# Mamba2 SSD and a low-rank mixer in one kernel: the first batch's products in another order, V loaded packed, and identity products in TensorE's first waits

## The chip, the cores and the metric

The kernel runs on one core of a Trainium2 chip. The metric is the device time of one execution in microseconds (us). The engines are named as the profile names them: PE is TensorE, PEld its weight load, DVE is VectorE, ACT is ScalarE, POOL is GpSimd, and SP issues the loads and stores.

## The reference

Two stages, cut to what matters. Inputs: x is (4, 8, 768, 32), a is (4, 8, 768), B and C are (4, 8, 768, 16); U, V and the two weight matrices of the mixer come as float64.

```python
# stage 1: a state-space scan per batch and head, chunk by chunk
L = exp(cum[:, None] - cum[None, :]) * causal        # cum: running sum of log a
y = ((C @ B.T) * L) @ x  +  (C @ state) * exp(cum)
state = exp(sum(log_a)) * state + (B * decay).T @ x
# stage 2: tokens x channels, x is (4, 768, 256)
u = x + ((x.T @ U) @ V).T                            # U 768x32, V 32x768
out = u + relu(u @ w_ch1) @ w_ch2                    # w_ch1 256x1024, w_ch2 1024x256
```

## The kernel before

A batch is cut into six chunks of 128 tokens, and these into three pairs; there are four batches, so twelve pairs, numbered 0 to 11. For each pair k the code has a row of small functions, and the order in which they are called is the order of every engine's queue: nothing reorders it later.

- `prep(k)` (L285): B and C times their decays, on DVE (Bs, Cs). `turn(k, c)` (L318): four TensorE transposes of Bs and Cs for one chunk, and ACT's copy of them to T. `gram(k)` (L330): C B^T, 16 products in four row groups at a time, into the tile `g`, which has only one buffer. `mask(k)` (L341): the causal mask over g on DVE, giving M, two instructions.
- `decayed(k)` (L305) on POOL gives bd; `state(k)` (L351): TensorE products of bd and x into A; `update(k)` (L370): the state S on DVE, and on POOL its spread form `wide`.
- `ychannel(k)` (L391): y as state term (L404, T and wide) plus chunk term (L412, x and M), into the single buffer `y`, copied by ACT to yT. `ytokens(k, c, n)` (L420): y turned back to tokens by TensorE, copied to ytok.
- The mixer of a batch (L433) is a list of pieces: `project` (L438, the U products, which add up over the chunks), `mixed` (L451, V products into g and DVE's add to yT, L460), 16 `up` pieces (L462; half the tokens and 128 of the 1024 hidden columns each, four passes of L467, then a relu) and six `down` pieces (L474). `some(n)` calls the next n pieces.

The TensorE works on float32; a full product shows as two passes, a transpose as one. The PSUM tiles are `w` with three buffers, `g` and `y` with one each.

U, V and the weights arrive as float64, read as pairs of 32-bit words. `to_fp32` (L241) turns them into float32 in two halves: e and top on DVE with rest and power on ACT, then three DVE instructions. `convert(n)` takes the next n halves of a list in the order U, V, four parts of w1, four of w2; `convert_ahead()` takes the first half of one weight and the second half of the one before. Thus their places in DVE's and ACT's queues are written out by hand as well. V is loaded four times over, into 32 partitions each: the rows of V4 are what the V products need (L130 to L132).

Loads stand in SP's queue in the order of L124 to L146: a, B and C of pair 0, U, x of pair 0, B and C of pair 1, x of pair 1, B and C of pair 2, V, the first part of w1, x of pair 2, and so on.

The first batch (pairs 0 to 2) has no other mixer to run beside it; its order is written out at L524 to L567, and that of the mixer of batch 0 beside pairs 3 and 4 at L570 to L597. From pair 3 on a loop (L602) sets the order.

Of the kernel before, what the change touches and what calls it, by code (L numbers as in the profile page):

```python
# [9 lines left out]
FP32 = mybir.dt.float32  # L10
# [10 lines left out]
def kernel(  # L21
# [27 lines left out]
    nc = tc.nc  # L49
    P = 128  # L50
# [38 lines left out]
    def load_bc(k):  # L89
        b, q = pairs[k]  # L90
        bc = bc_sb[k] = raw.tile([P, 2, 2, NH, N], FP32, tag="bc", name="bc")
        for c in range(2):
            sl = ts(2 * q + c, P)
            nc.sync.dma_start(out=bc[:, 0, c], in_=B[b, :, sl, :].rearrange("h s n -> s h n"))
            nc.sync.dma_start(out=bc[:, 1, c], in_=C[b, :, sl, :].rearrange("h s n -> s h n"))
# [7 lines left out]


    U_sb = const.tile([P, NC, RK], FP32)
    V4 = const.tile([P, HS], FP32)
    w1 = const.tile([P, NCB, DF], FP32)
    w2 = const.tile([P, NM, DM], FP32)
# [16 lines left out]
    load_words(U_sb, U2.rearrange("(c p) r -> p c r", p=P))  # L125
    load_x(0)
    load_bc(1)
    load_x(1)
    load_bc(2)
    t = words_of(V4[:, None])  # L130
    for q in range(4):
        nc.sync.dma_start(out=t[ts(q, RK)], in_=V2[:, ts(q % 2, S)])  # L132
    quarter = WCOLS // NCB
    for k in range(DF // quarter):
        load_words(w1[:, :, ts(k, quarter)],
# [41 lines left out]
    bias = const.tile([P, 1], FP32)  # L177
    nc.vector.memset(bias, -896.0 * 2.0 ** 23)


    la = const.tile([P, NB, NC, NH], FP32)
    R = NB * NH * NC // 2
    la_ps = bank("w", 2, R)
    for g in range(2):
        nc.tensor.transpose(out=la_ps[:, g], in_=a_sb[:, g], identity=ident[:R, :R])
    for b in range(NB):
        g, o = divmod(b * NH * NC, R)
        nc.vector.tensor_scalar(
            out=la[:, b].rearrange("p c h -> p h c"),
            in0=la_ps[:, g, o:o + NH * NC].rearrange("p (h c) -> p h c", h=NH),  # L190
            scalar1=1e-6, scalar2=1.0, op0=ALU.max, op1=ALU.min)
# [83 lines left out]
    bds = [const.tile([P, 2 * NH, 2, N], FP32, name=f"bd{i}") for i in range(2)]  # L275
    for t in bds:
        nc.gpsimd.memset(t, 0.0)
    st = {}
    yT, ytok = {}, {}

# [37 lines left out]
    def turn(k, c):  # L318

        s = st[k]  # L320
        tp = bank("w", 4, P)
        for i, name in enumerate(("Bs", "Cs")):
            flat = s[name].rearrange("p h v n -> p (h v n)")
            for g in range(2):
                nc.tensor.transpose(out=tp[:, 2 * i + g], in_=flat[:, ts(2 * c + g, P)],  # L325
                                    identity=ident)
        s["T", c] = T = att.tile([P, 4, P], FP32, tag="T", name="T", bufs=4)
        nc.scalar.copy(out=T, in_=tp)  # L328

    def gram(k):  # L330
# [183 lines left out]
    def some(n):  # L514
        for _ in range(min(n, len(pieces))):
            pieces.pop(0)()

    one, others = slice(0, 1), slice(1, NB)
    yT[0] = mix.tile([P, NCB, S], FP32, tag="yT", name="yT")
    ytok[0] = mix.tile([P, NC, DM], FP32, tag="ytok", name="ytok")  # L520
# [1 line left out]
    project = pieces.pop(0)  # L522

    decays(one)  # L524
    prep(0, 2)
    turn(0, 0)
    turn(0, 1)
# [2 lines left out]
    convert(1)  # L530
    gram(0)
    state(0)
    mask(0)
    prep(1)
    update(0)
    decayed(1)
    turn(1, 0)
    turn(1, 1)
    convert(1)
    ychannel(0)  # L540
    gram(1)
    state(1)
    prep(2)
    mask(1)
    decayed(2)
    turn(2, 0)
    turn(2, 1)
    update(1)
    ytokens(0, 0, 2)
    project(0, 2)  # L550
    convert(1)
    gram(2)
    ychannel(1)
    state(2)
    mask(2)
    update(2)
    convert(1)
    ytokens(1, 0, 2)
    project(2, 4)
    convert(2)  # L560
    ychannel(2, True)
    ytokens(2, 0, 1)
    project(4, 5)
    ytokens(2, 1, 1)
    project(5, 6)
    convert(1)
    some(1)  # L567


    some(1)  # L570
    convert_ahead()
    some(2)
    decays(others)
    keep(others)
    convert_ahead()
    some(4)
    convert_ahead()
    some(3)
    convert_ahead()
    some(2)  # L580
    prep(3)
    decayed(3)
    convert_ahead()
    some(1)
    turn(3, 0)
    turn(3, 1)
    some(1)
    convert_ahead()
    some(1)
    convert_ahead()  # L590
    gram(3)
    state(3)
    mask(3)
    update(3)
    some(1)
    prep(4)
    decayed(4)  # L597
    assert not halves
# [66 lines left out]
```

## Time and profile before

| | us |
|---|---|
| median of 3 runs | 272.89 (272.67 to 273.1) |
| the profiled execution | 275.54 |
| its span, first to last instruction | 273.8 |
| TensorE busy | 254.0 (93% of the span) |
| DVE busy | 102.2 (37%) |
| ACT busy | 68.6 (25%) |
| POOL busy | 30.3 (11%) |

The profile comes from one execution. Its page has the busy time of each engine, the span in slices, and the chain that ended last: at each step the work that released it, followed back from the end. TensorE carries 90% of that chain. The clock that the throttle granted to TensorE is given per stretch as a share of 2.4 GHz; 0.50 is 1.2 GHz.

### The profile page before, as it was taken

What the parts mean: (1) busy time and instruction counts of PE and PEld (TensorE: products, weight loads), DVE (VectorE), ACT (ScalarE), POOL (GpSimd) and SP (SyncE); (2) the same over time, 40 slices, a digit from 0 to 9 for tenths busy, and PEclk for the clock granted to TensorE, in tenths of its full rate; (3) what the DMA queues carried; (4) which work ended last, traced back from release to release, by engine and by line L of the source; (5) the groups of instructions that cost most, each with busy time, mean ns of one, the idle gap of its engine ahead of it and who ended that gap; (6) DMA issues with size and microseconds to landing.
All of it is one profiled execution on the core that took longest, in us unless ns stands there. A gap on an engine that the chain in (4) does not pass through costs nothing.

```text
span 273.8 us, 5204 instructions
## 1 busy us (share of the span) xinstructions
PE 254.0 (93%) x2250; PEld 191.2 (70%) x2250; DVE 102.2 (37%) x194; ACT 68.6 (25%) x143; POOL 30.3 (11%) x53
## 2 busy tenths in 40 slices
PE   2878779997799999999999999999999999999994
PEld 1857536564688887666778887666688876558883
DVE  3487943997443353063430413161600121120000
ACT  5314436674202200313221101222111101211110
POOL 4031100000640330012110300010000000000000
PEclk9999977999799999999999999999999999999999
DMA  6999747999983100100000010100000101000011
GB/s 96 119 188 258 130 162 126 117 89 119 111 93 45 60 4 0 57 2 0 2 1 2 4 56 0 60 2 0 2 0 0 60 0 57 2 0 0 0 60 57
DMA packets 81463, 14.66 MB, mean 54 GB/s; under 512 B 76000, under 2 KB 79264, under 8 KB 81440
## 3 DMA queue, kind: packets, MB, share of 16 engines
q1 hardware_dynamic: 81440, 14.33, 32.5%
q8 instruction: 18, 0.29, 0.5%
q14 instruction: 5, 0.04, 0.1%
HBM read 11.17 MB, written 3.15 MB: 52 GB/s over the span
## 4 chain that ended last, share of the span: by engine, by line
PE 90%; DVE 3%; ACT 3%; issue 1%; DVEq 0%; ACTq 0%
PE w L467 31%; PE w L483 30%; PE y L412 5%; PE g L338 5%; PE w L325 5%; PE y L404 4%; PE w L479 3%; PE w L445 2%; PE w L427 2%; PE g L456 1%; DVE M L347 1%; PE w L362 1%; ACT ytok L430 1%; DVE Bs L297 1%; ACT L214 0%
## 5 line engine op out<-in xcount | busy, mean ns | idle before, releaser
L467 PE MATMUL w<-yT,w 128*128 128x384 f32 x256 | 89.4, 502 | 0.9 <-DVE yT L460 0.7
L483 PE MATMUL w<-w,gT 128*128 128x256 f32 x384 | 86.9, 379 | 0.0
L483 PEld LDWEIGHTS w<-w,gT 128*128 128x128 f32 x384 | 71.1, 190 | 8.7
L467 PEld LDWEIGHTS w<-yT,w 128*128 128x128 f32 x256 | 48.3, 195 | 33.1 <-issue 3.3
L347 DVE TENSOR_TENSOR M<-g,causal 128x1024 int32<-128x1024 int32 x24 | 28.2, 1219 | 34.5 <-PE g L338 34.5
L472 ACT ACTIVATE gT<-w 128x384 f32<-128x384 f32 x40 | 19.6, 490 | 57.9 <-PE w L467 57.9
L485 ACT COPY o<-w 128x256 f32<-128x256 f32 x24 | 8.9, 372 | 90.9 <-PE w L483 90.9
L470 DVE TENSOR_SCALAR gT<-w 128x384 f32<-128x384 f32 x24 | 13.4, 557 | 44.5 <-PE w L467 44.3
L386 POOL TENSOR_TENSOR wide<-S,rmask 128x256 f32<-128x256 f32 x20 | 12.8, 655 | 141.8 <-DVE S L381 93.4
L430 DVE COPY ytok<-w 128x512 f32<-128x512 f32 x9 | 6.2, 689 | 33.0 <-PE w L427 33.0
L328 ACT COPY T<-w 128x512 f32<-128x512 f32 x24 | 13.6, 588 | 19.7 <-PE w L325 19.4
L325 PE MATMUL w<-ident,Bs 128*128 128x128 f32 x48 | 10.3, 301 | 6.9 <-DVE Bs L297 6.9
L338 PE MATMUL g<-T 32*128 32x128 f32 x384 | 15.4, 301 | 0.0
L460 DVE TENSOR_TENSOR yT<-g,yT 128x384 f32<-128x384 f32 x16 | 7.8, 549 | 20.2 <-PE g L456 20.2
L412 PE MATMUL y<-M,x 128*32 128x128 f32 x384 | 14.8, 299 | 0.5 <-ACT yT L416 0.5
L338 PEld LDWEIGHTS g<-T 32*128 32x128 f32 x384 | 13.0, 203 | 2.9 <-issue 2.8
L325 PEld LDWEIGHTS w<-ident,Bs 128*128 128x128 f32 x48 | 6.6, 152 | 9.9 <-issue 7.0
L412 PEld LDWEIGHTS y<-M,x 128*32 128x32 f32 x384 | 10.8, 119 | 2.6 <-ACT yT L416 0.8
L404 PEld LDWEIGHTS y<-T,wide 128*128 128x128 f32 x80 | 11.0, 202 | 1.5 <-issue 0.2
L404 PE MATMUL y<-T,wide 128*128 128x128 f32 x80 | 11.8, 290 | 0.0
L418 ACT COPY yT<-y 128x512 f32<-128x512 f32 x11 | 6.4, 586 | 19.7 <-PE y L412 19.7
L325 PE MATMUL w<-ident,Cs 128*128 128x128 f32 x48 | 10.3, 300 | 0.5 <-DVE Cs L297 0.5
(71 smaller groups left out, 166.7 us busy)
## 6 DMA issues: line engine op xcount, KB each, us to landing
words<-in_moe_w_ch_dram SPq DMA_DIRECT2D x8, 512.0 KB, 5.7
x<-in_x_dram SPq DMA_DIRECT2D x24, 128.0 KB, 3.9
out_dram<-o SPq DMA_DIRECT2D x8, 384.0 KB, 2.5
bc<-in_B_dram SPq DMA_DIRECT2D x24, 64.0 KB, 4.0
bc<-in_C_dram SPq DMA_DIRECT2D x24, 64.0 KB, 3.7
words<-in_moe_V_dram SPq DMA_DIRECT2D x4, 96.0 KB, 3.3
words<-in_moe_U_dram SPq DMA_DIRECT2D x1, 192.0 KB, 3.6
a_sb<-in_a_dram SPq DMA_DIRECT2D x1, 96.0 KB, 2.1
```

Of the source, the lines that this page charges most:

```text
L325: nc.tensor.transpose(out=tp[:, 2 * i + g], in_=flat[:, ts(2 * c + g, P)], identity=ident)
L328: nc.scalar.copy(out=T, in_=tp)
L338: nc.tensor.matmul(out=g_ps[:, r, c, g], lhsT=T[rows, g], rhs=T[rows, 2 + g], start=True, stop=True, skip_group_check=True)
L347: nc.vector.tensor_tensor(out=M[:, :, c].bitcast(INT32), in0=g_ps[:, :, c].bitcast(INT32), in1=causal[:, None, None, :].to_broadcast(sh), ...
L386: nc.gpsimd.tensor_tensor(out=wide, in0=new[:, :, None, :].to_broadcast(wide.shape), in1=rmask[:, None, :, None].to_broadcast(wide.shape), ...
L404: nc.tensor.matmul(out=y[:, c, g], lhsT=wide[:, g].rearrange("p r d -> p (r d)"), rhs=s["T", c][:, 2 + g], start=fresh, stop=False, skip_g ...
L412: nc.tensor.matmul(out=y[ts(r, Q), c, g], lhsT=x_sb[k][:, c, 4 * g + r], rhs=s["M"][:, r, c, g], start=False, stop=True, skip_group_check= ...
L430: copy(out=ytok[b][:, c:c + n].rearrange("p c (g d) -> p c g d", g=2), in_=t)
L467: nc.tensor.matmul(out=g, lhsT=w1[:, n, ts(m, P)], rhs=uT[:, n, ts(k, HS)], start=(n == 0), stop=(n == NCB - 1))
L470: nc.vector.tensor_relu(gT[k][:, m], g)
L472: nc.scalar.activation(gT[k][:, m], g, AF.Relu)
L483: nc.tensor.matmul(out=o, lhsT=gT[k][:, m, ts(j, P)], rhs=w2[:, m], start=False, stop=(m == NM - 1), skip_group_check=True)
```

## The change

The order of the first batch is written anew. C B^T of a pair (`gram`) now stands ahead of the preceding pairs' y; y of pair 0 comes behind the transposes of pair 2, and y of pairs 1 and 2 behind the C B^T of pair 2. The U products (`project`) stand behind the last y. V is loaded once, as four quarters of its columns on four groups of 32 partitions (Vq, half the bytes), converted in that form, and spread to V4's layout by two TensorE products with a 0/1 matrix (`twice`, made by POOL from the identity) and an ACT copy (`spread`). Its load stands ahead of those of pair 2's B and C and of pair 1's x. A function `warm(n)` issues n products of the identity with itself into a tile that nothing reads; it is called four times, with 3, 2, 7 and 8. The tile T has six buffers instead of four. Two more conversions stand ahead of the mixer's add, and behind it the `up` pieces and the conversions are grouped otherwise.

```diff
-    load_x(1)
-    load_bc(2)
-    t = words_of(V4[:, None])
-    for q in range(4):
-        nc.sync.dma_start(out=t[ts(q, RK)], in_=V2[:, ts(q % 2, S)])
+    t = words_of(Vq[:, None])
+    for q in range(4):
+        nc.sync.dma_start(out=t[ts(q, RK)], in_=V2[:, ts(q, HS)])
+    load_bc(2)
+    load_x(1)
...
+    def warm(n, tag="w"):
+        t = bank(tag, P) if tag == "w" else bank("g", 4, 4 * P)[:, 0, :P]
+        for _ in range(n):
+            nc.tensor.matmul(out=t, lhsT=ident, rhs=ident, start=True, stop=True)
+    warm(3, "g")
     la = const.tile([P, NB, NC, NH], FP32)
...
         nc.tensor.transpose(out=la_ps[:, g], in_=a_sb[:, g], identity=ident[:R, :R])
+    warm(2, "g")
...
+    twice = const.tile([P, 2, 2, 2 * RK], FP32)
+    for j in range(2):
+        nc.gpsimd.tensor_copy(
+            out=twice[:, :, j].rearrange("p i (a r) -> p i a r", a=2),
+            in_=ident.rearrange("p (a i r) -> p i a r", a=2, i=2))
...
+    def spread():
+        v = bank("w", 2, HS // 2)
+        for i in range(2):
+            nc.tensor.matmul(out=v[:, i], lhsT=twice[:, i], rhs=Vq, start=True, stop=True)
+        nc.scalar.copy(out=V4, in_=v)
...
     decays(one)
+    warm(7, "g")
     prep(0, 2)
...
     state(0)
+    warm(8)
     mask(0)
...
-    convert(1)
-    ychannel(0)
     gram(1)
+    convert(2)
     state(1)
     prep(2)
-    mask(1)
-    decayed(2)
     turn(2, 0)
     turn(2, 1)
+    mask(1)
     update(1)
+    decayed(2)
+    ychannel(0)
+    gram(2)
+    state(2)
+    convert(2)
+    update(2)
     ytokens(0, 0, 2)
+    ychannel(1)
+    mask(2)
+    spread()
+    convert(1)
+    ychannel(2)
+    convert(1)
     project(0, 2)
+    ytokens(1, 0, 2)
+    ytokens(2, 0, 2)
     convert(1)
-    gram(2)
-    ychannel(1)
-    state(2)
-    mask(2)
-    update(2)
-    convert(1)
-    ytokens(1, 0, 2)
     project(2, 4)
-    convert(2)
-    ychannel(2, True)
-    ytokens(2, 0, 1)
-    project(4, 5)
-    ytokens(2, 1, 1)
-    project(5, 6)
+    project(4, 6)
     convert(1)
     some(1)
-    some(1)
-    convert_ahead()
-    some(2)
+    for _ in range(3):
+        some(2)
+        convert_ahead()
     decays(others)
     keep(others)
...
     gram(3)
     state(3)
     mask(3)
     update(3)
-    some(1)
+    some(2)
     prep(4)
```

In TensorE's queue at the program's start stood before (la are the logs of a, ref0 and ref1 the matrices of the decay sums):

```order
L185 MATMUL w_225<-ident_197,a_sb_72 128x96 x2
L209 MATMUL w_248<-la_224,ref0_214 128x48
L209 MATMUL w_248<-la_224,ref1_215 128x48
L325 MATMUL w_260<-ident_197,Bs_254 128x128 x2
L325 MATMUL w_260<-ident_197,Cs_255 128x128 x2
```

and now stands

```order
L185 MATMUL g_225<-ident_198 128x128 x3
L193 MATMUL w_230<-ident_198,a_sb_72 128x96 x2
L185 MATMUL g_233<-ident_198 128x128 x2
L218 MATMUL w_259<-la_229,ref0_215 128x48
L218 MATMUL w_259<-la_229,ref1_216 128x48
L185 MATMUL g_265<-ident_198 128x128 x7
L340 MATMUL w_279<-ident_198,Bs_273 128x128 x2
L340 MATMUL w_279<-ident_198,Cs_274 128x128 x2
```

so three identity products come first, two stand behind the transposes of a, and seven between the decay sums and the first transposes of Bs.

In TensorE's queue between the state products of pairs 1 and 2 and the second U product stood before:

```order
L404 MATMUL y_362<-T_272,wide_337 128x128 x2
L412 MATMUL y_362<-M_328,x_85 32x128 x16
L338 MATMUL g_382<-T_350 128x128 x8
L338 MATMUL g_382<-T_357 128x128 x8
L362 MATMUL w_399<-x_93,bd1_242 32x32 x16
L325 MATMUL w_424<-ident_197,Bs_416 128x128 x2
L325 MATMUL w_424<-ident_197,Cs_417 128x128 x2
L325 MATMUL w_431<-ident_197,Bs_416 128x128 x2
L325 MATMUL w_431<-ident_197,Cs_417 128x128 x2
L427 MATMUL w_448<-ident_197,yT_245 128x128 x4
L445 MATMUL w_454<-ytok_246,U_sb_74 32x128 x8
L338 MATMUL g_471<-T_429 128x128 x8
```

and from the state products of pair 1 on stands now:

```order
L377 MATMUL w_415<-x_104,bd1_250 32x32 x16
L340 MATMUL w_436<-ident_198,Bs_432 128x128 x2
L340 MATMUL w_436<-ident_198,Cs_433 128x128 x2
L340 MATMUL w_443<-ident_198,Bs_432 128x128 x2
L340 MATMUL w_443<-ident_198,Cs_433 128x128 x2
L419 MATMUL y_464<-T_291,wide_365 128x128 x2
L427 MATMUL y_464<-M_356,x_86 32x128 x16
L353 MATMUL g_484<-T_441 128x128 x8
L353 MATMUL g_484<-T_448 128x128 x8
L377 MATMUL w_501<-x_109,bd0_249 32x32 x8
L442 MATMUL w_526<-ident_198,yT_256 128x128 x4
L419 MATMUL y_532<-T_385,wide_456 128x128 x2
```

The state term (L404, now L419) and chunk term (L412, now L427) of y(0) moved from ahead of C B^T of pair 1 to behind the transposes of pair 2; g of pair 2 (g_484) comes ahead of y(1) (y_532), and no U product stands here any more.

In DVE's queue around the mask of pair 2 (M_519 before, M_554 now) stood before:

```order
L347 TENSOR_TENSOR M_420<-g_382,causal_239 128x4x256 x2
L381 SCALAR_TENSOR_TENSOR S_438<-S_339,kept_237,w_399 128x32 x2
L381 SCALAR_TENSOR_TENSOR S_443<-S_438,kept_237,w_399 128x32 x2
L257 TENSOR_SCALAR e_463<-words_101 128x384
L259 TENSOR_SCALAR top_464<-words_101 128x384
L347 TENSOR_TENSOR M_519<-g_471,causal_239 128x4x256 x2
L381 SCALAR_TENSOR_TENSOR S_522<-S_443,kept_237,w_510 128x32 x2
L264 SCALAR_TENSOR_TENSOR rest_466<-top_464,rest_466 128x384
L266 SCALAR_TENSOR_TENSOR power_465<-words_101,power_465 128x384
L268 SCALAR_TENSOR_TENSOR V4_75<-rest_466,power_465 128x384
L257 TENSOR_SCALAR e_544<-words_106 128x512
L259 TENSOR_SCALAR top_545<-words_106 128x512
```

and now stands:

```order
L362 TENSOR_TENSOR M_450<-g_387,causal_247 128x4x256 x2
L396 SCALAR_TENSOR_TENSOR S_453<-S_367,kept_245,w_415 128x32 x2
L396 SCALAR_TENSOR_TENSOR S_458<-S_453,kept_245,w_415 128x32 x2
L273 SCALAR_TENSOR_TENSOR rest_410<-top_408,rest_410 128x192
L275 SCALAR_TENSOR_TENSOR power_409<-words_94,power_409 128x192
L277 SCALAR_TENSOR_TENSOR Vq_75<-rest_410,power_409 128x192
L266 TENSOR_SCALAR e_513<-words_107 128x512
L268 TENSOR_SCALAR top_514<-words_107 128x512
L396 SCALAR_TENSOR_TENSOR S_521<-S_458,kept_245,w_501 128x32 x2
L362 TENSOR_TENSOR M_554<-g_484,causal_247 128x4x256 x2
L273 SCALAR_TENSOR_TENSOR rest_516<-top_514,rest_516 128x512
L275 SCALAR_TENSOR_TENSOR power_515<-words_107,power_515 128x512
```

so the second half of V's conversion, the first half of w1's first part and the last state update come ahead of the mask of pair 2.

## Rows read from the trace of the kernel before

**Rows 1.** Windows: stretch, length, each engine's busy us, PE clock, DMA share, GB/s.

```profile
75.00:273.80 198.80, 194.91 (x1644) 149.97 (x1636) 51.51 (x91) 34.23 (x73) 16.91 (x25) 1.00 0.09 22
```

**Rows 2.** Chain of work, the up products of batch 0 to its first down piece.

```profile
38.55 6.82 PE w L467 x12
...
46.99 13.17 PE w L467 x40
60.15 0.87 PE w L325 x8
...
71.30 0.76 PE y L404 x4
72.06 1.87 PE y L412 x32
73.92 1.49 PE g L338 x32
...
75.80 0.37 PE w L479 x2
```

**Rows 3.** Chain of work in order of time (start us, us, what), first batch.

```profile
6.88 1.97 PE w L325 x8
...
10.41 2.07 PE g L338 x32
...
15.60 2.05 PE w L325 x8
17.65 0.85 PE y L404 x4
18.51 1.79 PE y L412 x32
20.30 1.10 PE g L338 x32
...
26.18 1.09 PE y L404 x8
27.27 1.05 PE y L412 x32
...
33.12 0.69 PE y L412 x16
```

**Rows 4.** Windows of 2 us, the granted clock behind the POOL column.

```profile
42.00:44.00 2.00, 2.00 (x5) 1.09 (x4) 0.49 (x1) 1.18 (x3) 0.00 (x0) 0.50 0.38 94
...
72.00:74.00 2.00, 2.00 (x37) 1.52 (x36) 0.00 (x0) 0.04 (x2) 0.68 (x2) 0.50 1.34 138
```

**Rows 5.** Timeline: copy, conversion on ACT, and the wait ahead of pair 4's transposes.

```profile
29.68 0.59 ACT L430 COPY ytok<-w 128x512 f32<-128x512 f32 x1 [0.75 <-PE w L427]
...
37.06 0.72 ACT L262 ACTIVATE power<-e,bias 128x512 int32<-128x512 int32 x1
...
63.79 1.17 PE L338 MATMUL g<-T 32*128 32x128 f32 x32
...
65.63 2.35 DVE L347 TENSOR_TENSOR M<-g,causal 128x1024 int32<-128x1024 int32 x2
...
69.50 0.41 PE L325 MATMUL w<-ident,Bs 128*128 128x128 f32 x2 [2.65 <-DVE Bs L297]
```

**Rows 6.** Timeline (start us, us, engine, line), decay sums and loads.

```profile
4.17 1.09 PE L209 MATMUL w<-la,ref 128*128 128x48 f32 x4 [0.61 <-ACT la L193]
...
9.05 1.46 SPq L102 DMA_DIRECT2D x<-in_x_dram  x2
...
13.83 2.00 SPq L132 DMA_DIRECT2D words<-in_moe_V_dram  x4
```

**Rows 7.** Issues of loads, landing us at the end: second half of pair 1's x.

```profile
x<-in_x_dram SPq DMA_DIRECT2D x1, 128.0 KB, 4.3
```

**Rows 8.** Windows: DVE from mask(0) to mask(2), and what followed mask(2).

```profile
12.50:26.25 13.75, 10.20 (x201) 8.26 (x200) 11.51 (x20) 4.50 (x8) 3.77 (x6) 1.00 1.04 220
28.57:31.69 3.12, 2.02 (x27) 1.59 (x28) 2.99 (x8) 1.95 (x4) 0.77 (x1) 1.00 0.63 83
```

More of the change, by code (lines that the diff above doesn't have):

```diff
@@ L105 @@
     U_sb = const.tile([P, NC, RK], FP32)
+    Vq = const.tile([P, HS // 2], FP32)
     V4 = const.tile([P, HS], FP32)
@@ L326, in turn @@
                                     identity=ident)
-        s["T", c] = T = att.tile([P, 4, P], FP32, tag="T", name="T", bufs=4)
+        s["T", c] = T = att.tile([P, 4, P], FP32, tag="T", name="T", bufs=6)
         nc.scalar.copy(out=T, in_=tp)
@@ L538 @@
     turn(1, 1)
-    convert(1)
-    ychannel(0)
     gram(1)
+    convert(2)
     state(1)
     prep(2)
-    mask(1)
-    decayed(2)
     turn(2, 0)
     turn(2, 1)
+    mask(1)
     update(1)
-    ytokens(0, 0, 2)
+    decayed(2)
[4 more added lines that the diff above has]
+    update(2)
+    ytokens(0, 0, 2)
+    ychannel(1)
[4 more added lines that the diff above has]
+    convert(1)
     project(0, 2)
+    ytokens(1, 0, 2)
+    ytokens(2, 0, 2)
     convert(1)
-    gram(2)
-    ychannel(1)
-    state(2)
-    mask(2)
-    update(2)
-    convert(1)
-    ytokens(1, 0, 2)
-    project(2, 4)
-    convert(2)
-    ychannel(2, True)
-    ytokens(2, 0, 1)
-    project(4, 5)
-    ytokens(2, 1, 1)
-    project(5, 6)
+    project(2, 4)
+    project(4, 6)
     convert(1)
     some(1)
-    some(1)
-    convert_ahead()
-    some(2)
+    for _ in range(3):
+        some(2)
+        convert_ahead()
     decays(others)
     keep(others)
[L575 to L578, printed above, removed]
+    some(2)
     convert_ahead()
@@ L583 @@
     convert_ahead()
-    some(1)
+    some(2)
     turn(3, 0)
@@ L589 @@
     some(1)
-    convert_ahead()
     gram(3)
@@ L594 @@
     update(3)
-    some(1)
+    some(2)
     prep(4)
```

## The prediction

> **What bounds the kernel now.** I began with long stretches of the span. From 75 us on TensorE is busy 194.91 of 198.80 us at the full clock [rows 1]. Only DVE's conversions and the first batch stand before that, so the change can only move the moment at which this dense part begins; in before the first `down` piece (L479) starts at 75.80 [rows 2].
>
> Next comes the chain of waits of the first batch [rows 3]. Eight transposes take 1.97 and 2.05 us there, a C B^T group (32 passes of L338) 2.07, a y group of 32 passes of L412 1.79. Behind 20.3 the same work takes 1.10 (L338) and 1.05 (L412), and eight transposes 0.87 [rows 2, 3]. The clock column shows 1.00 from the start, but these durations are those of the lower level (1.2 GHz against 2.4), so I go by durations. TensorE had worked almost without a gap from 15.60 when they changed. The clock falls twice more: the column shows 0.50 at 42 to 44 and at 72 to 74 [rows 4]. Before the first fall lay the small steps and copies between the last y, which ended at 33.81, and the first L467 at 38.55 [rows 2, 3]; before the second TensorE had waited 2.65 us for one operand [rows 5].
>
> So before 75.8 four things are lost: a late start of the `up` products (38.55), their half clock, the wait at 69.50, and the half clock behind that.
>
> **The change part by part.** *The identity products* are two passes each. A full 128-column pass at half clock costs 0.85/4 = 0.213 us (L404) [rows 3], so a product 0.43. The three and the two lie ahead of operands that come later anyway (the first decay product starts at 4.17) [rows 6]; they push it by 0.2 at most, hidden since ACT is still loading its table then and takes the decays later. The seven stand between the decay products, which end at 5.26 [rows 6], and the first transposes, which start at 6.88 [rows 3]: 7 x 0.43 = 3.0 us, to 8.3 at half clock. If the clock rises among them they end at 7.6. I take 8.0, a step that TensorE runs 1.1 later than now, paid back by the transposes at 0.87 instead of 1.97, the four decay pairs of `keep` (1.56 now, 10.41 - 8.85) at about 0.9 and L338 at 1.10: gram(0) ends at 11.0 instead of 12.48. The eight products of the second burst lie behind state(0), where TensorE waits for DVE until 15.60: after gram(0) ends at 12.48 come mask(0) (a pair of L347 is 2.35) [rows 5] and 0.77 to the first transpose. At full clock, 8 x 2 x 0.136 (L404 26.18) = 2.2 us, they cost nothing; at half clock, 3.4 us, up to 1.0.
>
> The Trainium skill ("TensorE: Matmul & The Clock Gate", Part 1) says that the ramp to the full clock costs less than 1% of a typical kernel's span, which would be 2.7 us here. The rows don't agree: the first batch alone has lost 1.10 + 1.18 (transposes), 0.97, 0.30 and 0.74 us to the half clock, 4.3 in all, and my sum goes by them.
>
> *Loads.* On SP's queue x1 moves behind V and the loads of bc2. Now x1 is issued from 9.05 to 10.51, bc2 to 13.8, V in 2.00 us after it [rows 6]. In the new order x1 is issued from 9.05 + (1.0 to 2.0 for V, half as many bytes) + 3.3 for bc2 = 13.4 to 14.4, its second half 0.7 later, and lands 4.3 after that [rows 7]: 18.4 to 19.4. state(1) needs it, and stands in TensorE's queue behind gram(1) and ahead of turn(2). Turn(1) can start at 11.0 + 2.35 + 0.77 = 14.1; with its transposes 0.87, the copy of T 0.6 (as ytok's of the same shape) [rows 5] and L338 1.10 gram(1) ends near 16.7. **So a new wait of some 2 us for x1 appears**, queued ahead of all of the third pair's work. It is as long as what took the clock down at 69.5, so whether the clock stays up over it decides much.
>
> *The order of the first batch.* y(0) goes behind turn(2), y(1) and y(2) behind gram(2), all U products behind the last y. DVE's chain from mask(0) to mask(2): 11.51 busy us now; ahead of mask(2) come, in addition, the V half, the first half of w1's first words and the last update, 2.99 us as they are now [rows 8]; V packed saves up to half of its part (0 to 1.6). From mask(0) at 11.1: mask(2) starts at 24.0 to 25.6 and ends, 2.35 later, at 26.4 to 28.0; I take 27.3. TensorE's own chain from x1: 18.4 + 0.39 (32 state passes, 75.41 to 75.80) = 18.8, turn(2) 0.87, y(0) 0.55 + 1.05, gram(2) 1.10, state(2) 0.2, ytokens(0) half of 0.87, y(1) 1.09 + 1.05, the V spread 4 x 1.5 x 0.136 = 0.8: 25.9 at full clock; with turn(2), y(0) and gram(2) at half clock 1.1 + 1.0 + 1.0 more, 29.0, and 29.3 with the later bound of x1's landing partly under DVE's chain. y(2) starts between 27.3 and 29.3, I take 28.3, the middle.
>
> *From y(2) to the first up product.* y(2) itself 1.09 + 1.05. In before the last y ends at 33.81 and the first L467 starts at 38.55: 4.74 us of copies, U products, h and the add [rows 2, 3]. In the new order y(2) is not split, so whole copies of 0.59 [rows 5] take the place of halves, and in ACT's queue the two conversions of w1's second words stand ahead of the ytok copies (1.4 us, the second of the pair is the 0.72 row) [rows 5]; the U products of pairs 0 and 1 run under these. I add 0.8: 5.5 us, between 4.7 and 6.7. First up product at 28.3 + 2.14 + 5.5 = 36.0. The conversions that DVE now has between mask(2) and the add (two second halves, two first halves) are some two stretches like the 2.99 one [rows 8]: 27.3 + 6.0 = 33.3, ahead of the add at 35.4, so they cost nothing. **First term: 38.55 - 36.0 = 2.55.**
>
> *The ups.* The first 12 passes took 6.82, the next 40 took 13.17, that is 3.95 for 12 [rows 2]. With the full clock kept through the handover: **2.87**.
>
> *The wait at 69.50.* gram(3) ends at 64.96, but mask(3) starts at 65.63 only, since the last conversion is still on DVE; TensorE then waits 2.65 for Bs [rows 5]. The change puts two up products there instead of one (4 x 13.17/40 = 1.32 more cover), and DVE reaches that point some 3 us further ahead in its conversions, so mask(3) starts 0.5 earlier: **1.8**; 0.85 of the wait is left.
>
> *Behind it*, with 0.85 instead of 2.65 of idling the clock should stay: L404 0.76 - 0.55, L412 1.87 - 1.05, L338 1.49 - 1.10 [rows 2, 3]: **1.43**.
>
> Sum: 2.55 + 2.87 + 1.8 + 1.43 = 8.65 us. The profiled execution took 275.54 us (span 273.8), 1% over the 272.89 of the runs; it would take 266.9, and the runs 272.89 - 8.65 = **264.2**.
>
> **Rivals.** (1) *The clock is up by the first transposes and survives the x1 wait.* Then y(2) starts at 26.5 to 27.3 and the ups at 34.6: 10.05 us, 262.8. For: with the bursts TensorE's early waits are filled. Against: the 2 us at state(1).
>
> (2) *The identity products don't do what they say*: the clock stays low through them. Then turn(0) starts at 8.3, gram(0) ends near 14.0, the eight products end at 18.1, and turn(1) starts there, 2.5 later than now; x1 costs nothing then. gram(1) ends at 21.6, mask(1) at 24.2, mask(2) at 29.8; ups at 29.8 + 7.6 = 37.4, first term 1.1: 265.7. For: seven and eight products are 3 us each, and the rise in before needed more work than that. The Trainium skill (the same page and part) says that the number of products at the lower clock changes from run to run of one kernel; no row here shows a second run, and the sum does not use it.
>
> (3) *The clock falls in the handover all the same.* TensorE still waits there for the ytok copies, for pT and for the add. For: that is what it did in before; against: two wait-and-copy rounds fewer. The second term goes: 267.1. Together with (2): 268.6.
>
> (4) *Slower.* The x1 wait takes the clock down and it stays down to the ups. All work from turn(2) to h at half clock: 1.1 (turn(2)) + 1.0 (y(0)) + 1.0 (gram(2)) + 0.2 + 0.4 + 2.1 (y(1)) + 0.8 + 2.1 (y(2)) and about 2 for the handover's products = 10.6 on top of rival 1's start, ups at 45.2, the ups' second term lost, and only 1.8 + 1.43 won: -6.65 + 3.2, that is 3.4 slower, 276.3. It turns into a loss once the ups start later than 38.55 + 3.2 = 41.8 at half clock. Against: y(1), spread and y(2) are 5 us of full products in a row, as at 15.60 to 20.3.
>
> **How the numbers follow.** Forecast 0.45 (263 to 265.5), rival 1 0.15, rival 2 0.15, rival 3 0.17, rival 4 0.06; 0.02 for losses and gains that cancel out. The range goes from 261.8 (rival 1 with the handover at 4.7) to 268.6 (rivals 2 and 3 together). About 0.2% is what a measurement of this kernel can tell from no change. Faster 0.92, same 0.02, slower 0.06.
>
> **What would show it.** The first eight transposes near 0.9 us from about 8; gram(0) ended by 11; a wait of 1 to 3 us of state(1) for x1; mask(2) ended at 26.4 to 28.0 and y(2) behind it; the first up product at 34.6 to 37.4 with passes of 0.33; a wait below 1.2 ahead of turn(4); first `down` product near 67. Wrong if the ups start after 38.5, if they run at 0.64 a pass, or if the last wait is again over 2 us.

## The result and the profile after

The changed kernel takes 265.75 us (median of four executions: 264.68, 265.0, 266.49, 266.68) against 273.0 of before beside it (272.67 to 273.19): 0.973 of it, 95% interval 0.969 to 0.978, so 7.25 us faster. The prediction was 264.2 with a range of 261.8 to 268.6: the range holds the time, which is 1.55 us above the point.

The profiled execution took 264.68 us (span 263.0). Its page begins:

```profile
span 263.0 us, 5281 instructions
## 1 busy us (share of the span) xinstructions
PE 251.1 (95%) x2294; PEld 192.2 (73%) x2294; DVE 100.7 (38%) x194; ACT 67.6 (26%) x142; POOL 30.6 (12%) x55
...
PEclk9999999999999999999999999999999999999999
```

TensorE has 44 instructions more than before and is busy 95% of a shorter span; the row of its clock shows no stretch below full speed. Line numbers have moved: the transposes are L340 (L325 before), C B^T L353 (L338), y L419 and L427 (L404, L412), the `up` products L482 (L467), the first `down` pieces L494 and L498 (L479 begins them before), the identity products L185, the state products L377, the V spread L537.

The timeline of TensorE in the first batch (start us, us, engine, line, operation, count, and in brackets the idle time ahead with what ended it) answers [rows 3]:

```profile
4.98 2.78 PE L185 MATMUL g<-ident 128*128 128x128 f32 x14
7.60 0.38 PE L340 MATMUL w<-ident,Bs 128*128 128x128 f32 x2
...
9.44 1.17 PE L353 MATMUL g<-T 32*128 32x128 f32 x32
...
13.79 0.41 PE L340 MATMUL w<-ident,Bs 128*128 128x128 f32 x2 [0.80 <-DVE Bs L312]
...
17.99 0.33 PE L377 MATMUL w<-x,bd 128*32 128x32 f32 x16 [1.37 <-DMA x<-in_x_dram]
18.68 0.33 PE L377 MATMUL w<-x,bd 128*32 128x32 f32 x16 [0.36 <-DMA x<-in_x_dram]
18.95 0.44 PE L340 MATMUL w<-ident,Bs 128*128 128x128 f32 x2
...
26.30 1.13 PE L419 MATMUL y<-T,wide 128*128 128x128 f32 x8
```

A pair of transposes takes 0.38 us from 7.60 on: by the durations the clock rose among the seven identity products (the column of the clock shows 1.00 all along), and the work that ran at half of it before now takes what it takes later in the program. The new wait, state(1) for x1, is there (1.37 and 0.36), and the clock stays up behind it. The chain of waits (start us, us, what) shows what y(2) stands on and answers [rows 2]:

```profile
22.16 0.48 POOL bd L326
...
22.68 0.33 PE w L377 x16
...
25.51 0.85 PE w L537 x4
26.35 1.08 PE y L419 x8
27.43 1.05 PE y L427 x32
...
33.92 8.01 PE w L482 x24
...
61.12 0.88 PE w L340 x6
61.99 0.45 PE y L419 x4
62.44 1.01 PE y L427 x32
63.45 1.10 PE g L353 x32
...
64.94 0.37 PE w L494 x2
```

y(2) (L419, L427) starts behind the V spread (L537): TensorE works without a gap from state(2) at 22.68 to the end of y(2) at 28.48, and state(2) had to have `bd`, which POOL finished at 22.64. The first `up` product starts at 33.92 instead of 38.55; 24 passes take 8.01 (12 took 6.82 before); what follows turn(4) runs at 0.45, 1.01 and 1.10 instead of 0.76, 1.87 and 1.49; and the first `down` piece starts at 64.94 instead of 75.80. These 10.86 us are the whole difference of the two profiled executions (275.54 - 264.68). They split into 4.63 (start of the ups), 2.82 (6.82 - 12 x 8.01/24), 1.87 (wait ahead of turn(4), 2.65 in [rows 5], 0.78 now, below) and 1.56 (behind it), 10.88 in all. From there on the two kernels do the same.

The timeline of TensorE and DVE shows that wait, and two places of the first batch (mask(2), and the add ahead of the first `up` product):

```profile
60.19 0.41 PE L340 MATMUL w<-ident,Bs 128*128 128x128 f32 x2 [0.78 <-DVE Bs L312]
...
23.76 2.34 DVE L362 TENSOR_TENSOR M<-g,causal 128x1024 int32<-128x1024 int32 x2
...
33.31 1.95 DVE L475 TENSOR_TENSOR yT<-g,yT 128x384 f32<-128x384 f32 x4 [0.91 <-PE g L471]
```

The medians differ by 7.25 only, because executions of either kernel come in kinds, by the mean granted clock recorded for them: two of after at 1.00 (264.68, 265.0) and two at 0.993 and 0.994 (266.49, 266.68); those of before lie between 271.8 and 274.2 or, at 0.976 to 0.979, above 275.1. The profiled one of before is of the last kind. Where these kinds come from is part of the experiments. Below, an execution "at 1.00" is one with that recorded clock.

### The profile page after: what moved, and what is told of

The parts are those of the page before. It is cut to its first block, busy times and chain, and to the rows that moved or that the text cites. A ratio compares the mean times of both kernels' runs of the same rounds, so it can differ in the third digit from the quotient of the medians.

```text
span 263.0 us, 5281 instructions
## 1 busy us (share of the span) xinstructions
PE 251.1 (95%) x2294; PEld 192.2 (73%) x2294; DVE 100.7 (38%) x194; ACT 67.6 (26%) x142; POOL 30.6 (12%) x55
## 4 chain that ended last, share of the span: by engine, by line
PE 87%; SPq 4%; DVE 3%; issue 1%; DMA 1%; ACT 1%; POOL 1%; DVEq 0%
PE w L498 32%; PE w L482 31%; PE y L427 4%; PE g L353 4%; PE y L419 3%; PE w L340 3%; PE w L494 3%; PE w L460 2%; SPq L95 2%; PE w L442 2%; DVE M L362 1%; PE g L471 1%; DMA bc<-in_B_dram 1%; PE w L377 1%; SPq L94 1%
## 5 line engine op out<-in xcount | busy, mean ns | idle before, releaser
L482 PE MATMUL w<-yT,w 128*128 128x384 f32 x256 | 86.6, 490 | 1.1 <-DVE yT L475 0.7
L498 PE MATMUL w<-w,gT 128*128 128x256 f32 x384 | 86.9, 379 | 0.0
L498 PEld LDWEIGHTS w<-w,gT 128*128 128x128 f32 x384 | 71.1, 190 | 8.7
L482 PEld LDWEIGHTS w<-yT,w 128*128 128x128 f32 x256 | 47.0, 190 | 31.3 <-DVE yT L475 1.5
L401 POOL TENSOR_TENSOR wide<-S,rmask 128x256 f32<-128x256 f32 x20 | 12.6, 645 | 128.3 <-DVE S L396 88.6
L353 PE MATMUL g<-T 32*128 32x128 f32 x384 | 14.1, 283 | 0.2 <-ACT T L343 0.2
L353 PEld LDWEIGHTS g<-T 32*128 32x128 f32 x384 | 11.8, 186 | 2.9 <-issue 2.3
L427 PE MATMUL y<-M,x 128*32 128x128 f32 x384 | 13.0, 276 | 0.0
L419 PEld LDWEIGHTS y<-T,wide 128*128 128x128 f32 x80 | 10.3, 191 | 1.4 <-issue 0.2
L419 PE MATMUL y<-T,wide 128*128 128x128 f32 x80 | 10.9, 276 | 0.0
L427 PEld LDWEIGHTS y<-M,x 128*32 128x32 f32 x384 | 9.8, 109 | 1.4
L340 PE MATMUL w<-ident,Bs 128*128 128x128 f32 x48 | 9.3, 275 | 1.6 <-DVE Bs L312 1.6
L326 POOL TENSOR_TENSOR bd<-bc,FD 128x256 f32<-128x256 f32 (+1 forms) x12 | 7.4, 619 | 25.6 <-ACT kept L247 20.3
L340 PE MATMUL w<-ident,Cs 128*128 128x128 f32 x48 | 9.3, 275 | 0.6 <-DVE Cs L312 0.5
```

Source lines behind the costliest of these rows:

```text
L353: nc.tensor.matmul(out=g_ps[:, r, c, g], lhsT=T[rows, g], rhs=T[rows, 2 + g], start=True, stop=True, skip_group_check=True)
L401: nc.gpsimd.tensor_tensor(out=wide, in0=new[:, :, None, :].to_broadcast(wide.shape), in1=rmask[:, None, :, None].to_broadcast(wide.shape), ...
L419: nc.tensor.matmul(out=y[:, c, g], lhsT=wide[:, g].rearrange("p r d -> p (r d)"), rhs=s["T", c][:, 2 + g], start=fresh, stop=False, skip_g ...
L427: nc.tensor.matmul(out=y[ts(r, Q), c, g], lhsT=x_sb[k][:, c, 4 * g + r], rhs=s["M"][:, r, c, g], start=False, stop=True, skip_group_check= ...
L482: nc.tensor.matmul(out=g, lhsT=w1[:, n, ts(m, P)], rhs=uT[:, n, ts(k, HS)], start=(n == 0), stop=(n == NCB - 1))
L498: nc.tensor.matmul(out=o, lhsT=gT[k][:, m, ts(j, P)], rhs=w2[:, m], start=False, stop=(m == NM - 1), skip_group_check=True)
```

## Experiments

Experiments 1 to 4 ran beside one set of runs of before (273.19), 5 to 8 beside another (275.19), 9 and 10 beside a third (273.0), 11 and 12 beside a fourth (272.67). Experiments 9 to 12 ran on another chip than 1 to 8. Where medians are set against the 265.75 of after, that is over several sets; the lowest executions of before agree over them (271.81 to 271.94). In the second set four of the seven executions of before are at 0.979, so a ratio to its median is some 0.8% lower than it would be in the others.

**1. Without the identity products.**

```diff
-    warm(3, "g")
-    warm(2, "g")
-    warm(7, "g")
-    warm(8)
```

> The changed kernel without its twenty identity products; all else as in it. Theory A (they bring the full clock to the first batch): the first transposes run at about 1.97 us for eight again, the first mask starts near 12.4 instead of 10.68, and the up products start near 36 instead of 33.9; time 267.5 to 268.5. Rival (DVE and the loads set the first batch, the clock there costs nothing): 265 to 266, as the changed kernel.

266.51 us (266.44 to 268.15), 0.976 of before (0.970 to 0.982). TensorE in the timeline:

```profile
10.31 2.09 PE L351 MATMUL g<-T 32*128 32x128 f32 x32
...
15.57 0.66 PE L338 MATMUL w<-ident,Bs 128*128 128x128 f32 x2 [2.58 <-DVE Bs L310]
...
17.55 2.09 PE L351 MATMUL g<-T 32*128 32x128 f32 x32
19.57 0.66 PE L375 MATMUL w<-x,bd 128*32 128x32 f32 x32
...
35.73 2.20 PE L480 MATMUL w<-yT,w 128*128 128x384 f32 x6 [0.68 <-DVE yT L473]
```

Both C B^T groups are at half clock (2.09), the full clock comes at 21, and the wait for x1 is gone, since TensorE is late itself. The ups start 1.81 us later than in after. So the products bring 1.8 us between the two profiled executions (266.49 - 264.68), which both keep the clock afterwards, and 0.76 between the medians: 266.51 lies between what the two theories expected. All four executions are at 0.998 here, so none lost the clock later, while two of after's four are at 0.993 and 0.994; the medians set these kinds against each other. The larger part of the gain is the rest of the change.

**2. The identity products alone, in before.**

```diff
 (before)
+    warm(3, "g")
+    warm(2, "g")
+    warm(7, "g")
+    warm(8)
```

> The kernel before with the four bursts of identity products and nothing else of the change. Theory A: the first mask starts near 10.7 instead of 12.5; pair 2's B and C, which land near 17, take back a part; the old order of the y and U products keeps the rest of its waits: 271 to 272, at least two thirds of the gain then come from the new order. Rival (the identity products are the main part): 268 or less.

271.12 us (268.89 to 272.76), 0.990 of before (0.986 to 0.994). gram(0) runs at 9.78 and the ups start at 35.15, 3.4 earlier than in before, but their first 12 passes take 5.79 and the wait ahead of turn(4) is 2.65 as it was. Windows of TensorE (stretch, length, busy us of PE, PEld, DVE, ACT, POOL, the clock, DMA share, GB/s):

```profile
36.00:38.00 2.00, 2.00 (x5) 1.09 (x4) 2.00 (x6) 0.00 (x0) 0.00 (x0) 0.50 1.01 384
...
66.00:68.00 2.00, 2.00 (x10) 2.00 (x10) 0.96 (x1) 1.02 (x2) 2.00 (x3) 0.50 0.97 100
```

Both falls of the clock that [rows 4] show are still there, the first of them shorter (0.50 to 38.5 instead of 44, some 3.4 us instead of 6.8). That they go altogether belongs to the new order. Here, in the old one, the products alone bring the ups 3.4 us forward, nearly twice what they bring in the new one.

**3. x1 ahead of V on the queue** (and V's first conversion half moved behind update(1)).

```diff
     load_bc(1)
+    load_bc(2)
+    load_x(1)
     t = words_of(Vq[:, None])
...
-    load_bc(2)
-    load_x(1)
```

> The changed kernel with the loads in the order B and C of pair 2, x of pair 1, V, and the first half of V's conversion moved behind the state update of pair 1. Theory A (DVE's chain sets y of pair 2, TensorE's wait for x of pair 1 is covered by it): the wait of the state products for x (1.37 + 0.36 us) falls below 0.3, the up products start 0 to 0.5 earlier, 265 to 266. Rival (the wait for x is on the path): 1.5 us less, 263.5 to 264.5.

266.39 us (264.73 to 267.47), 0.973 (0.967 to 0.979). state(1) doesn't wait any more (it starts at 17.85), and little comes of it: turn(2) waits for DVE (0.40) and state(2) for POOL (0.70). In the profiled execution the clock rose some 2 us later than in after, mask(0) starts 1.30 later (11.98) and the ups 0.79 later (34.71); from mask(0) to y(2) it is 0.5 us shorter, about what the conversion half that was moved takes on DVE (0.42). The wait for x1 lies beside a chain of DVE (mask(1), update) and POOL (`wide`, `bd`) that state(2) waits for. At 1.00 the one execution is as long as after's (264.73).

**4. One `up` product ahead of turn(4) instead of two** (the other goes ahead of gram(3)).

```diff
-    some(1)
+    some(2)
     gram(3)
...
     update(3)
-    some(2)
+    some(1)
     prep(4)
```

> The changed kernel with one up piece instead of two between the state update of pair 3 and the products of pair 4, the other one ahead of C B^T of pair 3. Theory A: TensorE's wait for Bs of pair 4 grows by one piece, 1.3 us, and the clock may fall behind it: 267 to 268.5. Rival (the wait ends with DVE, which starts earlier when the piece is moved ahead): no change, 265 to 266.

268.41 us (267.64 to 269.85), 0.981 (0.976 to 0.987): 2.66 more than after. TensorE's timeline, and a window (columns as in 2):

```profile
58.40 1.56 PE L482 MATMUL w<-yT,w 128*128 128x384 f32 x4
62.02 0.64 PE L340 MATMUL w<-ident,Bs 128*128 128x128 f32 x2 [2.06 <-DVE Bs L312]
```

```profile
62.00:64.00 2.00, 1.69 (x7) 1.32 (x8) 1.92 (x2) 0.27 (x1) 2.00 (x3) 0.51 1.20 145
```

The wait grows from 0.78 to 2.06, that is by about the 1.3 us of the four passes moved (4 x 0.334), and the clock falls behind it, as it did in before. A single call moved by a few lines is worth more than the identity products.

**5 and 6. Before and after once more,** unchanged, for a second look at the clock.

> The kernel before, unchanged, for a second profile: its timed runs have a mean granted clock near 0.992 and a span near 271.3, the profiled one 0.979 and 273.8. Theory A (the profiled execution lost the clock once more than most): this profile has 0.99 to 0.994 and only one of the two stretches at 0.50, and the up products or y of pair 3 run at the full clock. Rival (the difference lies elsewhere): both stretches are there.

> The changed kernel, unchanged, for a second profile: its timed runs are either near 264.8 (clock 1.00) or near 266.6 (0.993). Theory A (in the second kind the clock falls once, in the handover to the up products or ahead of pair 4's transposes): if this execution is of that kind, one stretch of some 3.4 us at 0.50 stands at 30 to 38 or at 59 to 65 and the time is 266.4 to 266.8; otherwise the chain is that of the first profile, 264.5 to 265.1, and nothing is decided.

Before took 275.21 us at a clock of 0.979, with the falls at the same two places (0.50 from 37 to 43 and from 71 to 74); after took 265.19 at 1.00, which decides nothing. So the profiled execution of before was no one-off: over all sets 12 of 46 executions of before took 275 us or more. But of the 42 with a recorded clock 30 are at 0.991 or more: most executions lose less of the clock, and my sum took two of its terms from one that lost more.

**7. The last conversions of ACT behind the U products,** to shorten the handover; the loop over the ups begins with single ones.

```diff
     ychannel(2)
-    convert(1)
     project(0, 2)
     ytokens(1, 0, 2)
     ytokens(2, 0, 2)
-    convert(1)
...
-    for _ in range(3):
-        some(2)
+    for n in (1, 1, 2, 2):
+        some(n)
         convert_ahead()
```

> The changed kernel with the two ACT conversions of w1's second part moved from ahead of the ytok copies to behind the U products' copy, and what follows them shifted by one place. Theory A (the 1.2 us of these two on ACT's queue are on the path from the last y to the ups): the ups start 0.9 to 1.2 earlier after y of pair 2, time 264.4 to 265.2. Rival (DVE's conversions or the add are next at once): no change, 265.3 to 266.3.

268.24 us (268.12 to 269.47), 0.980 (0.972 to 0.987), worse than after: its four executions are all above after's (264.68 to 266.68). The handover from y(2) to the ups is 0.5 shorter, and then:

```profile
34.12 8.01 PE L482 MATMUL w<-yT,w 128*128 128x384 f32 x24 [0.75 <-DVE yT L475]
...
45.58 9.70 PE L482 MATMUL w<-yT,w 128*128 128x384 f32 x24 [2.01 <-ACT FC L226]
```

ACT does the conversions later and so comes late with FC, the factors of the later decays: TensorE waits 2.01 us, and the next 24 passes take 9.70 instead of 8.01, at half clock in part. The gain was given back eleven microseconds on.

**8. Identity products in the handover and ahead of turn(4) as well.**

```diff
     ytokens(2, 0, 2)
+    warm(3)
     convert(1)
...
+    warm(1)
     some(1)
+    warm(2)
...
     some(2)
+    warm(3)
     prep(4)
```

> The changed kernel with nine more identity products that nobody reads: three behind the ytok transposes, one ahead of and two behind the V products, three ahead of pair 4's transposes. Theory A (the slower half of the runs loses the clock in one of these waits): all runs near 264.8 to 265.2, clock 1.00, spread below 0.8. Rival 1 (the products are in the way): 0.5 to 1.0 slower than 265.75. Rival 2 (the clock falls elsewhere): two kinds of runs again.

267.7 us (266.4 to 269.11), 0.977 (0.968 to 0.985). The two executions at 1.00 have spans of 264.7 and 265.1, 1.7 more than after's 263.0 and 263.3. In the profiled execution the handover takes 6.25 us (32.10 to 38.35) instead of 5.44: products that nobody reads stand ahead of products that somebody waits for. It (0.987) lost its clock at a place where I had put none (a window of 2 us):

```profile
20.00:22.00 2.00, 2.00 (x25) 1.94 (x23) 2.00 (x6) 0.59 (x1) 0.12 (x1) 0.50 0.94 266
```

That is behind the wait of state(1), 3.17 us long here.

**9. 7 and 8 together** (without the products behind the last ytokens).

```diff
 (as in 7, and)
+    warm(1)
     some(1)
+    warm(2)
...
     some(2)
+    warm(3)
     prep(4)
```

> The changed kernel with the two ACT conversions of w1's second part behind the U products' copy, and six more identity products that nobody reads (one ahead of and two behind the V products, three ahead of pair 4's transposes). Theory A (both the conversions' 1.2 us and the lost clock are on the path): 263.6 to 264.4, clock 1.00 in nearly all runs. Rival (one of the two gives the other's gain back): 265 to 266.

265.95, 267.98 and 268.33 us, and 271.19, 271.23 and 271.4 at 0.972 to 0.979; the first three are 0.978 of before (0.971 to 0.985). Worse than after either way. The profiled execution, 271.4 us, has the 2.00 us for FC again (at 48.70), with half clock behind it, and half clock behind state(1)'s wait too (2.72 and 0.82 us). The first is the price of experiment 7; the second lies ahead of everything that this edit changes.

**10. V in full again,** loaded four times over and converted at 384 columns a row as in before; the spread is gone.

```diff
-    t = words_of(Vq[:, None])
+    t = words_of(V4[:, None])
...
-        nc.sync.dma_start(out=t[ts(q, RK)], in_=V2[:, ts(q, HS)])
+        nc.sync.dma_start(out=t[ts(q, RK)], in_=V2[:, ts(q % 2, S)])
...
     mask(2)
-    spread()
```

> The changed kernel with V loaded four times over and converted whole as before (384 columns), without the spread products and their copy. Theory A (DVE's chain to the mask of pair 2 sets y of pair 2): the chain grows by V's half, 0.5 to 1.6 us, and loads of pair 2 come 0 to 0.4 later; TensorE saves 0.85 of spread; 266 to 267.3. Rival (TensorE's own chain sets it): 0 to 0.9 faster than 265.75.

266.58 us (266.17 to 267.0), 0.975 (0.969 to 0.980): 0.8 more than after in the medians, 1.2 to 1.5 between the executions at 1.00 (266.17 against 264.68 and 265.0). TensorE in the timeline:

```profile
8.15 0.64 PE L340 MATMUL w<-ident,Bs 128*128 128x128 f32 x2
...
24.15 0.33 PE L377 MATMUL w<-x,bd 128*32 128x32 f32 x16 [0.66 <-POOL bd L326]
...
27.77 1.13 PE L419 MATMUL y<-T,wide 128*128 128x128 f32 x8 [0.80 <-ACT yT L433]
```

The ups start at 35.40, 1.48 later than in after, but 0.86 of that is there before V is touched: the clock rose later (a pair of transposes takes 0.64), and mask(0) starts at 11.54 instead of 10.68. V in full adds 0.6: from mask(0) to state(2) it is 12.6 us instead of 12.0. The 0.85 of the spread that TensorE saves is lost to a wait for yT (0.80). So packing V pays some 0.6 us in the profiled pair; the two intervals of the ratio overlap almost wholly and don't show it.

**11. Three `up` products ahead of turn(4).**

```diff
-    some(1)
     gram(3)
...
     update(3)
-    some(2)
+    some(3)
     prep(4)
```

> The changed kernel with three up pieces instead of two between the state update of pair 3 and the products of pair 4, the third taken from ahead of C B^T of pair 3. Theory A (there TensorE still waits 0.77 for Bs and 0.52 for Cs of pair 4, set by DVE's mask behind C B^T of pair 3): the first wait goes, the second falls to some 0.3: 0.9 to 1.0 less than the changed kernel in runs of the same clock, 263.7 to 264.2 at 1.00, and fewer runs that lose the clock; median 264 to 265.3. Rival (the copies of T of pair 3 are not covered any more, or the mask starts no earlier): 265.3 to 266.7.

**263.79 us** (263.59 to 266.06), 0.968 of before (0.963 to 0.974): the best kernel of this study, 2 us below after in the medians and 1.1 between executions at 1.00 (263.59 to 263.89). Of the waits ahead of turn(4), 0.78 for Bs and 0.52 for Cs in after, 0.19 is left:

```profile
57.95 4.14 PE L482 MATMUL w<-yT,w 128*128 128x384 f32 x12
61.92 0.38 PE L340 MATMUL w<-ident,Bs 128*128 128x128 f32 x2
62.49 0.44 PE L340 MATMUL w<-ident,Cs 128*128 128x128 f32 x2 [0.19 <-DVE Cs L312]
```

Its profiled execution is of the other kind (266.06 us, 0.994) and so shows one execution of that kind. Up to turn(3) it is the same program as after. First SP's queue in the timeline of after:

```profile
9.34 1.97 SPq L131 DMA_DIRECT2D words<-in_moe_V_dram  x4
...
14.49 1.44 SPq L102 DMA_DIRECT2D x<-in_x_dram  x2
```

And SP's queue and TensorE in experiment 11's, with a window behind them:

```profile
9.73 3.24 SPq L131 DMA_DIRECT2D words<-in_moe_V_dram  x4
...
15.37 1.75 SPq L102 DMA_DIRECT2D x<-in_x_dram  x2
...
19.18 0.33 PE L377 MATMUL w<-x,bd 128*32 128x32 f32 x16 [2.88 <-DVE Cs L312]
19.96 0.42 PE L377 MATMUL w<-x,bd 128*32 128x32 f32 x16 [0.45 <-DMA x<-in_x_dram]
20.31 0.69 PE L340 MATMUL w<-ident,Bs 128*128 128x128 f32 x2
...
36.59 1.24 PE L482 MATMUL w<-yT,w 128*128 128x384 f32 x3 [0.68 <-DVE yT L475]
```

```profile
20.00:22.00 2.00, 2.00 (x24) 1.94 (x25) 2.00 (x7) 0.54 (x1) 0.28 (x1) 0.51 1.12 255
```

V's four issues take 3.24 us instead of 1.97, one of them 1.62 instead of 0.42; x1 goes out 0.9 later and arrives later; state(1) waits 2.88 and 0.45 instead of 1.37 and 0.36; and the work behind it runs at half clock (0.69 a pair). The ups start 2.67 us later than in after: 1.28 by x1 (19.96 against 18.68) and some 1.5 by the clock (from there to the end of gram(2) 5.4 us instead of 3.9), less the 0.14 that state(2) waits for POOL in after. The profile names DVE's Cs as what ended the longer wait; in after state(1) starts ahead of the end of that Cs, so I take it to be x1 here too. The table has all nine profiled executions of this load order that reach this point with the clock up ("TensorE ready" is the start of state(1) less its wait).

| execution | V's issues | x1 issued | TensorE ready | wait of state(1), 1st and 2nd half | clock behind it |
|---|---|---|---|---|---|
| after | 1.97 | 14.49 | 16.62 | 1.37, 0.36 | 1.00 |
| after again (6) | 2.15 | 14.94 | 16.81 | 1.75, 0.44 | 1.00 |
| one up (4) | 1.97 | 14.77 | 16.80 | 1.40, 0.85 | 1.00 |
| late conversions (7) | 1.97 | 14.63 | 17.41 | 0.48, 1.11 | 1.00 |
| V in full (10) | 2.02 | 15.40 | 17.49 | 1.19, 0.56 | 1.00 |
| three, split (12) | 2.37 | 14.78 | 17.51 | 0.85, 0.35 | 1.00 |
| both (9) | 3.58 | 15.23 | 16.14 | 2.72, 0.82 | 0.50 |
| three ups (11) | 3.24 | 15.37 | 16.30 | 2.88, 0.45 | 0.50 |
| fill (8) | 3.93 | 15.85 | 16.18 | 3.17 | 0.50 |

They sort by the length of the wait and by V's issues, but just as well by when TensorE is ready, which goes with when the clock rose at the start: the first transposes begin at 6.81 to 7.28 in experiments 8, 9 and 11 and at 7.60 to 8.15 in the others. Of the 1.51 us by which 11's first wait is longer than after's, 0.32 is TensorE's earlier arrival and 1.19 is x1. No experiment changed one of these alone, so what of the two an execution owes its long wait to is not shown, and that the wait's length decides is read from this table only.

**12. Three ups, and pair 4's Bs and Cs in halves** (`prep(4, 2)`), against the last 0.19.

```diff
 (as in 11, and)
-    prep(4)
+    prep(4, 2)
```

> As the one with three up pieces, and Bs and Cs of pair 4 made chunk by chunk, as those of pair 0 are. Theory A: the wait for Cs goes as well, 0.2 to 0.4 less than with three pieces alone: 263.4 to 263.9 at clock 1.00, median 263.7 to 265. Rival (four smaller DVE instructions cost as much as they save): as with three pieces.

266.57 us (265.32 to 267.17), 0.977 (0.971 to 0.982): slower than 11; five of the six executions are at 0.990 to 0.994, two of the six in 11. The timeline of DVE and POOL shows a part of it:

```profile
58.86 0.53 DVE L312 TENSOR_TENSOR Bs<-bc,FB 128x256 f32<-128x256 f32 x1
59.32 0.83 DVE L312 TENSOR_TENSOR Cs<-bc,FC 128x256 f32<-128x256 f32 x1
59.83 0.80 POOL L326 TENSOR_TENSOR bd<-bc,FD 128x256 f32<-128x256 f32 x1
...
60.59 1.23 POOL L312 TENSOR_TENSOR Cs<-bc,FC 128x512 f32<-128x512 f32 x1
60.84 1.27 DVE L312 TENSOR_TENSOR Cs<-bc,FC 128x256 f32<-128x256 f32 x1
```

The same half takes 0.42 us at the start of the program, where POOL is idle, and 0.53 to 1.27 here, beside POOL's products. The Trainium skill ("GPSIMD Engine Reference", section 1, Specifications) says that POOL's way into SBUF is shared with DVE and that an instruction of DVE with two SBUF inputs contends with it; these rows agree. Turn(4) then waits 0.29 and 0.70 us, 0.8 more than in 11. Where the other executions lost the clock was not read.

## Why the prediction was right, and where its sizes were off

The steps, against the profiled execution of after:

| step of the prediction | predicted | measured |
|---|---|---|
| first transposes, eight of them | near 0.9 from about 8 | 0.9 from 7.60 |
| gram(0) ends | by 11 | 10.5 |
| state(1) waits for x1 | 1 to 3 (some 2) | 1.73 |
| mask(2) ends | 26.4 to 28.0 | 26.10 |
| y(2) starts | 27.3 to 29.3 | 26.30 |
| end of y(2) to the first up | 5.5 | 5.44 |
| first up product | 36.0 | 33.92 |
| a pass of the ups | 0.33 | 0.334 |
| wait ahead of turn(4) | 0.85 | 0.78 |
| first `down` piece | near 67 | 64.94 |

**The identity products** raise the clock among the seven in after, as the forecast had it; rival 2 (they don't) is wrong, though in experiments 3, 7, 10 and 12 the rise came only during the first transposes. I gave the early half clock 4.3 us in all. In the old order that was not far off: the products alone bring the ups 3.4 us forward (experiment 2). For the new order it was a mistake. There they bring 1.8 us, 0.7% of the span: without them mask(0) starts 1.79 us later (12.47 against 10.68) and y(2) 1.80 later (28.10 against 26.30), so what turn(1) and gram(1) lose at half clock behind mask(0), some 2 us, lies beside the chain of DVE and POOL and costs nothing. The rule of the Trainium skill that I weighed against my rows ("TensorE: Matmul & The Clock Gate", Part 1: under 1% of a typical span) fits the new order, and not the old one, where 3.4 us are 1.2%.

**The loads.** The wait for x1 came as predicted, and its length is what I had open: "whether the clock stays up over it decides much". Both answers occur. At 1.37 and 0.36 the clock stays, and that is rival 1, whose gain of 10.05 is near the 10.86 of the profiled pair. In the three profiled executions with 2.7 to 3.2 us for the first half it fell, and came back 3.5 to 7 us later, ahead of y(2); in experiment 11 the ups then start at 36.59, near the forecast's 36.0. My forecast lay between two kinds of executions. Rival 4, the loss, had its first half right (the clock falls behind the wait) and its second wrong (it does not stay down to the ups).

**First term** (2.55). Measured 4.63 at 1.00: I had let turn(2), y(0) and gram(2) run at half clock in one bound of y(2)'s start and taken the middle; at full clock y(2) starts at 26.30, near the 25.9 that I had added up for TensorE's own chain. The step that I had wrong is that y(2) comes behind mask(2): that mask ends at 26.10, and the chunk term, the first to read it, starts at 27.43. What sets y(2) is TensorE's work from state(2) on, and ahead of that POOL's `bd`, which my chains leave out: state(2) starts 0.14 us behind gram(2) in after and waits 0.23 to 0.70 for `bd` in experiments 3, 7, 10 and 12. In experiment 11's execution the term is 38.55 - 36.59 = 1.96.

**Second and fourth terms** (2.87 and 1.43). Against the profiled execution they measured 2.82 and 1.56. What failed is the last step: that the sum made on that execution may be taken from the median of the runs. It had lost the clock twice (0.979). The lowest executions of before in the four sets beside the experiments have spans of 269.8 to 270.1 instead of 273.8, two of them at 1.00 (270.1 and 270.0). So some 3.7 to 4.0 us of these 4.4 are not there to be won against them, if the difference is the two falls (none of them has a profile), and a median execution has lost part of it. Between the best of either kernel, 271.81 and 264.68, the gain is 7.13; the first and third terms as measured, 4.63 and 1.87, make 6.5 of it.

So that the point lies within 1.55 us of the time is in part luck: the first term was 2.08 too small, and the second and fourth were taken in full from a median that had lost only part of them. For the profiled execution the sum gave 266.9, and it took 264.68. The lower end of the range is also 0.2 lower than its own words give: 262.8 less 0.8 (5.5 - 4.7) is 262.0.

**Third term** (1.8). Measured 1.87, and experiments 4 and 11 confirm the step in both directions: 1.3 us less cover puts 1.3 on the wait and brings the clock down, 1.3 more takes the wait away.

**Handover and rival 3.** The step from y(2) to the ups was right to 0.1, and the clock did not fall in it in any profiled execution of the new order; rival 3 is wrong for these. DVE's additional conversions cost nothing, as predicted: DVE is idle 0.91 us ahead of the add. On ACT the order was right as it stands: experiment 7 shows what the conversions cost when they are moved.

What stays open: no execution of after itself at 0.993 or 0.994 has a profile. That this program can lose the clock behind state(1) is shown on experiments 8, 9 and 11, which are the same up to there. Experiment 3 still has two executions at 0.994, with x1 ahead of V; where these lose it isn't known, and why V's issues take 2 us in one execution and 3 to 4 in another isn't either. What makes the executions of before differ was read only in profiles at 0.979.

## What to carry to other kernels

Before a sum of terms is subtracted from a median, ask whether the profiled execution is a median one: a term read from a stretch at half clock counts only in executions that have it. A wait of TensorE on the path costs its length and, if the clock falls behind it, a second time; the shorter wait for x1, beside a longer chain, cost next to nothing (experiment 3). Real work moved in front of a wait (one call of `some`) brought 2.7 us here where products that nobody reads brought 0.76 in front of the first batch and cost 1.7 elsewhere. Before two profiled executions are subtracted, see whether the clock rose at the same moment in both: in experiments 3 and 10 that alone shifted the first batch by 1.30 and 0.86 us. And a conversion taken off the path must be followed to its next reader on the same engine's queue.

## What the runs showed of the hardware that I had not expected

- The clock rose at different times in the same first instructions: the 14 passes of the seven identity products took 1.88 us in experiment 8, 2.78 in after, 2.96 in after again and 3.32 in experiment 3, and a pair of passes of the first transposes took 0.38 us from the first pair on (7.60) in after, from the third on (8.82) in experiment 7 and in none of the four in experiment 3 (0.63, 0.63, 0.64 and 0.52 from 8.19), with the identity products in place in all of them.
- Four equal issues of V on SP's queue take 1.97 to 3.93 us, one of them up to 1.94 instead of 0.42, and with them the place of everything behind them on that queue.
- A recorded clock of 1.00 does not say that all work was at full speed: experiment 12's profiled execution is recorded at 1.00 with its first pair of transposes at 0.63 us instead of 0.38, and experiment 1's at 0.998 with both its first C B^T groups at half speed (2.09 us against 1.17).
